# Cosine attention and a GELU layer on one core: a new hand-written order for the first three batches

## The chip, the cores and the metric

The kernel runs on one core of a Trainium2 chip. The core has five engines that run side by side, each through its own instructions in their written order: PE (matrix products; its weight loads are listed apart as PEld), ACT (exponentials, logarithms, GELU, squares), DVE (elementwise work and reductions on vectors), POOL (elementwise work, and the issue of some transfers) and SP (issue of transfers alone). They wait for each other by semaphores. Data lies in an on-chip memory (SBUF); PE writes its results to eight accumulator banks (PSUM), which are used singly or in pairs. The metric is the device time of one execution in microseconds (us).

## The reference

Eight batches of 12 heads, 448 positions, head size 64. Queries and keys are normalised, a softmax over cosines at a temperature of 0.1 weighs the values, and the result goes through a layer with a GELU between two products.

```python
q_n = q / (np.linalg.norm(q, axis=-1, keepdims=True) + 1e-06)
k_n = k / (np.linalg.norm(k, axis=-1, keepdims=True) + 1e-06)
scores = np.matmul(q_n, k_n.transpose(0, 1, 3, 2)) / tau
scores = scores - np.max(scores, axis=-1, keepdims=True)
attn = np.exp(scores)
attn = attn / (np.sum(attn, axis=-1, keepdims=True) + 1e-09)
attn_out = np.matmul(attn, v)
x = attn_out.transpose(0, 2, 1, 3).reshape(B * S, H * D)   # 3584 x 768
h = x @ w_in                                               # 768 x 2048
g = 0.5 * h * (1.0 + erf(h / sqrt(2)))
out = g @ w_out                                            # 2048 x 768
```

## The kernel before

Four heads make a quad, so a batch has three quads: quads 0 to 2 are batch 0, quads 3 to 5 batch 1, quads 6 to 8 batch 2, and so on to 23. A quad's Q and K arrive as one tile `qk` (`load_qk`, on SP). Work on a quad is done by units: unit 0 and unit 1 are the two halves of quad 0, and from there unit n + 1 is quad n. So "quad 1" is unit 2.

A unit passes through these steps, each a small function: `square` (Q or K squared, on ACT, DVE or POOL as the call says), `reduce` (sums of squares, DVE), `logs` and `roots` (a logarithm and an exponential on ACT give the norm), `inverses` (DVE), `scale` (Q or K times the inverse norm, on DVE or POOL), and `transposes`. The latter run on PE with `copies` by DVE behind them for the first units, and as a transposing transfer on SP for later ones. Then `scores` (PE, tile `st`) and `exps` (ACT, tile `pt`) work through a quad in seven chunks, and `sums` and `values` (PE, tiles `sm` and `o`) use them. The sums become reciprocals on DVE (`turned`, `inverted`, `spread`), and `normalise` writes the batch's input `x` of the GELU layer. In place of `sums`, some quads add up their exps on POOL (`folded`) or DVE (`gather`).

The GELU layer of a batch is `mm` or `first` (PE, tiles `hp`: 16 tiles of six products each), `gelu` (ACT, to `g`), and the second product, cut into output pieces of 16 steps (tile `op`). `run(1)` does the next step of the next piece. Steps of a batch's pieces fill PE between the scores of the next batch. `table` loads ACT's set of functions: the exponential set or the GELU set. `spin` issues a filler product that nobody reads.

The weights `wi` come in parts (`load_wi(0)` to `load_wi(3)`, the last two halves of one), `wo` in four, and V in parts; POOL issues these transfers (`load_wi`, `load_wo`, `load_v`) between its other instructions.

What sets the order: for batches 0 to 2 the function `opening` is a list of calls, one line for each step, that fixes the order of every engine's instructions. No scheduler moves them. From the first product of batch 2 on (`first(2)`), loops with a rule for the spacing of scores set the order (`attention`, `first`). Units that share their logarithm and root are in one group (`groups`); units 5 and 6 (quads 4 and 5) are such a pair. `root2` holds the tiles for the roots.

The accumulator pairs `st0` and `st1` alternate between score tiles; `open_third` and `open_fourth` turn single banks into a third and fourth pair once quads 0 to 2 are done.

Of the kernel before, what the change touches and what calls it, by code (L numbers as in the profile page):

```python
# [16 lines left out]
def kernel(  # L17
# [462 lines left out]
    def upto(f, n, last=None):  # L480
        last = {load_qk: NG, load_v: NV, root: len(groups), load_wi: NQ + 1, load_wo: 4}.get(f, NU)
# [56 lines left out]
    def opening():  # L538
        load_qk(0)
        table(EXP_SET)  # L540
        load_qk(1)
        load_qk(2)
        spin(20)
        late_copy()
        load_qk(3)
        x_t[0] = xp.tile([128, KD, S], BF16, tag="x", name="x0")
        square(0, ((AC, Q),))
        square(0, ((AC, K),))
        reduce(0, Q)
        reduce(0, K)  # L550
        square(1, ((AC, Q),))
        load_v(0)
        logs(0)
        reduce(1, Q)
        roots(0)
        load_wi(0)
        square(1, ((AC, K),))
        inverses(0)
        square(2, ((AC, Q),))
        reduce(1, K)  # L560
        scale(0, ((GP, 1),))
        logs(1)
        reduce(2, Q)
        roots(1)
        scale(0, ((GP, 0),))
        spin(2)
        transposes(0, 1)
        square(2, ((AC, K),))
        inverses(1)
        spin(1)  # L570
        transposes(0, 0)
        square(3, ((AC, Q),))
        copies(0, 1)
        scale(1, ((GP, 0),))
        copies(0, 0)
        square(3, ((AC, K),))
        scale(1, ((GP, 1),))
        load_qk(4)
        spin(1)
        transposes(1, 0)  # L580
        reduce(2, K)
        scores(0, ((0, 0), (0, 1)))
        load_v(1)
        transposes(1, 1)
        copies(1, 0)
        logs(2)
        scores(0, ((0, 2), (0, 3)))
        roots(2)
        load_wi(1)
        exps(0, ((0, 0), (0, 1)))  # L590
        inverses(2)
        copies(1, 1)
        exps(0, ((0, 2), (0, 3)))
        spin(2)
        scores(0, ((0, 4), (0, 5)))
        scale(2, ((GP, 0),))
        reduce(3, Q)
        exps(0, ((0, 4), (0, 5)))
        spin(1)
        scores(0, ((1, 0), (1, 1)))  # L600
        reduce(3, K)
        exps(0, ((1, 0), (1, 1)))
        spin(1)
# [12 lines left out]
        exps(0, ((1, 4), (1, 5)))
        inverses(3)
        sums(0, (1,))
        scale(3, ((GP, 0),))
        copies(2, 1)  # L620
        sums(0, (2,))
        exps(0, ((0, 6), (1, 6)))
        sums(0, (3,))
        sums(0, (4,))
        scores(1, ((0, 0), (1, 0)))
        scores(1, ((0, 1), (1, 1)))
        sums(0, (5,))
        exps(1, ((0, 0), (1, 0)))
        sums(0, (6,))
        load_wi(2)  # L630
        transposes(3, 0)
        turned(0)
        exps(1, ((0, 1), (1, 1)))
        scores(1, ((0, 2), (1, 2)))
        values(0, (0,))
        scale(3, ((GP, 1),))
        load_wi(3)
        copies(3, 0)
        values(0, (1,))
# [3 lines left out]
        inverted(0)
        values(0, (3,))
        values(0, (4,))
        spread(0, 1)
        values(0, (5,))
        exps(1, ((0, 3), (1, 3)))
        scores(1, ((0, 4), (1, 4)))
        values(0, (6,))  # L650
        spread(0, 0)
        sums(1, (0,))
        square(4, ((GP, K),))
        exps(1, ((0, 4), (1, 4)))
        sums(1, (1,))
        scores(1, ((0, 5), (1, 5)))
        normalise(0, 0)
        transposes(3, 1)
        exps(1, ((0, 5), (1, 5)))
        scores(1, ((0, 6), (1, 6)))  # L660
        copies(3, 1)
        sums(1, (2,))
        square(4, ((GP, Q),))
        square(5, ((GP, Q),))
        square(5, ((GP, K),))
        load_wo(0)
        load_wo(1)
        exps(1, ((0, 6), (1, 6)))
        sums(1, (3,))
        sums(1, (4,))  # L670
        normalise(0, 1)
        scores(2, ((0, 0), (1, 0)))
        sums(1, (5,))
        exps(2, ((0, 0), (1, 0)))
        sums(1, (6,))
        scores(2, ((0, 1), (1, 1)))
        turned(1)
        values(1, (0,))
        values(1, (1,))
        exps(2, ((0, 1), (1, 1)))  # L680
        values(1, (2,))
        scores(2, ((0, 2), (1, 2)))
        inverted(1)
        values(1, (3,))
        values(1, (4,))
        spread(1, 0)
        values(1, (5,))
        exps(2, ((0, 2), (1, 2)))
        values(1, (6,))
        scores(2, ((0, 3), (1, 3)))  # L690
        sums(2, (0,))
        reduce(4, K)
        normalise(1, 0)
        exps(2, ((0, 3), (1, 3)))
        sums(2, (1,))
        scores(2, ((0, 4), (1, 4)))
        spread(1, 1)
        sums(2, (2,))
        scores(2, ((0, 5), (1, 5)))
        exps(2, ((0, 4), (1, 4)))  # L700
        values(2, (0,))
        values(2, (1,))
        exps(2, ((0, 5), (1, 5)))
        values(2, (2,))
        bank(0, 4)
        bank(0, 5)
        values(2, (3,))
        values(2, (4,))
        scores(2, ((0, 6), (1, 6)))
        exps(2, ((0, 6), (1, 6)))  # L710
        banks(0, 0, 1)
        mm(0, 4, 0, 2)
        sums(2, (3,))
        normalise(1, 1)
        square(6, ((GP, Q),))
        reduce(5, Q)
        reduce(4, Q)
        logs(4)
        sums(2, (4,))
        sums(2, (5,))  # L720
# [715 lines left out]
```

## Time and profile before

| what | value |
|---|---|
| median of 3 runs | 391.53 us |
| lowest and highest run | 390.82 and 393.38 us |
| profiled execution, span from first to last instruction (its only time in the profile) | 390.6 us |
| ACT's last exp of quad 2 ends | 32.42 us |
| batch 0's first product goes on without a break from | 33.3 us |
| batch 1's first product begins | 77.8 us |
| batch 2's first product begins | 129.9 us |

The profile has one line for each group of instructions: line of the code, engine, operation, what it writes and reads, count, and after the bar the busy time in all, the mean of one in nanoseconds, and the engine's idle time ahead of them with what ended it. A row of the timeline gives the start and the length in microseconds, the instruction, how many are merged in it, and in brackets the idle time before it. A row of the stretches gives the window, its length, and then busy time and count for PE, PEld, DVE, ACT and POOL, the granted clock, the share of the transfer engines, and GB/s. A row of the list of waits gives who waited for whom, the total, how often, and the longest.

### The profile page before, as it was taken

What the parts mean: (1) busy time and instruction counts of PE and PEld (TensorE: products, weight loads), DVE (VectorE), ACT (ScalarE), POOL (GpSimd) and SP (SyncE); (2) the same over time, 40 slices, a digit from 0 to 9 for tenths busy, and PEclk for the clock granted to TensorE, in tenths of its full rate; (3) what the DMA queues carried; (4) which work ended last, traced back from release to release, by engine and by line L of the source; (5) the groups of instructions that cost most, each with busy time, mean ns of one, the idle gap of its engine ahead of it and who ended that gap; (6) DMA issues with size and microseconds to landing.
All of it is one profiled execution on the core that took longest, in us unless ns stands there. A gap on an engine that the chain in (4) does not pass through costs nothing.

```text
span 390.6 us, 13166 instructions
## 1 busy us (share of the span) xinstructions
PE 382.6 (98%) x5820; PEld 236.6 (61%) x5820; DVE 273.0 (70%) x509; ACT 269.9 (69%) x391; POOL 248.7 (64%) x161
## 2 busy tenths in 40 slices
PE   7899999999999999999999999999999999999996
PEld 3444568555777656865567556775567555655674
DVE  4878439876778896879696896889685993670032
ACT  5895789857999958996678767997577646504300
POOL 4796950557998399969594794969595770910000
PEclk9999999999999999999999999999999999999999
DMA  8999999926899691889067490876045600130033
GB/s 265 264 262 229 176 191 329 254 56 157 179 203 299 112 217 69 185 158 275 5 172 130 120 243 2 185 131 118 3 91 81 154 9 2 44 82 2 7 79 83
DMA packets 64473, 54.85 MB, mean 140 GB/s; under 512 B 38688, under 2 KB 60320, under 8 KB 64416
## 3 DMA queue, kind: packets, MB, share of 16 engines
q1 hardware_dynamic: 54464, 41.79, 42.0%
q0 software_dynamic: 9568, 11.80, 18.5%
q8 instruction: 45, 0.74, 0.8%
q10 hardware_dynamic: 384, 0.43, 0.4%
q14 instruction: 12, 0.10, 0.1%
HBM read 45.61 MB, written 11.01 MB: 145 GB/s over the span
## 4 chain that ended last, share of the span: by engine, by line
PE 95%; DMA 2%; SPq 1%; ACT 1%; issue 0%; DVE 0%; ACTq 0%
PE hp L493 37%; PE op L427 36%; PE st L257 9%; PE o L346 8%; DMA qk<-in_k_dram 2%; PE op L451 1%; PE sm L323 1%; PE sm L332 1%; PE tp L236 1%; SPq L134 1%; ACT sq L173 0%; ACT pt L267 0%; PE spin L489 0%; DVE last L454 0%; ACT root L195 0%
## 5 line engine op out<-in xcount | busy, mean ns | idle before, releaser
L427 PE MATMUL op<-wo,g 64*64 64x384 bf16 x3456 | 167.1, 323 | 0.2 <-issue 0.2
L267 ACT ACTIVATE pt<-st 128x896 bf16<-128x896 f32 x168 | 147.2, 918 | 19.6 <-PE st L257 17.5
L493 PE MATMUL hp<-x,wi 128*128 128x448 bf16 x768 | 147.0, 353 | 0.0
L427 PEld LDWEIGHTS <-g 64*64 64x64 bf16 x3456 | 106.2, 107 | 40.9 <-issue 4.2
L493 PEld LDWEIGHTS <-wi 128*128 128x128 bf16 x768 | 74.3, 98 | 71.6 <-issue 3.2
L219 POOL TENSOR_TENSOR qkb<-qk,rn 128x896 bf16<-128x896 f32 (+1 forms) x49 | 80.4, 1662 | 46.0 <-DVE rn L203 37.9
L278 POOL TENSOR_TENSOR acc<-acc,pt 128x896 f32<-128x896 f32 x55 | 103.8, 1888 | 4.3
L436 DVE TENSOR_REDUCE ot<-op 128x384 f32<-128x768 f32 x50 | 47.3, 946 | 54.7 <-PE op L427 47.5
L1357 ACT ACTIVATE g<-hp 128x448 bf16<-128x448 f32 x96 | 46.2, 547 | 55.1 <-PE hp L493 55.1
L257 PE MATMUL st<-qkT 64*64 64x448 bf16 x672 | 62.8, 352 | 0.5 <-ACT pt L267 0.5
L183 DVE TENSOR_REDUCE nq<-sq 128x14 f32<-128x896 f32 (+1 forms) x50 | 50.4, 1036 | 13.6 <-ACT sq L173 7.1
L380 DVE TENSOR_TENSOR x<-o,rs 128x448 bf16<-128x448 f32 x48 | 27.6, 611 | 22.9 <-PE o L346 21.9
L175 POOL TENSOR_TENSOR sq<-qk 128x896 f32<-128x896 f32 x16 | 26.6, 1685 | 23.8 <-DMA qk<-in_q_dram 13.3
L346 PE MATMUL o<-pt,v 64*64 64x448 bf16 x672 | 39.5, 349 | 0.0
L290 DVE TENSOR_TENSOR acc<-acc,pt 128x896 f32<-128x896 f32 x30 | 33.0, 1099 | 1.0
L173 ACT ACTIVATE sq<-qk 128x896 f32<-128x896 f32 (+1 forms) x33 | 28.8, 901 | 4.4 <-DMA qk<-in_q_dram 3.2
L257 PEld LDWEIGHTS <-qkT 64*64 64x64 bf16 x672 | 23.1, 106 | 11.7 <-issue 3.7
L375 DVE STREAM_TRANSPOSE rs<-rc 128x448 f32<-128x448 f32 x48 | 28.1, 621 | 0.4
L278 POOL TENSOR_TENSOR acc<-pt 128x896 f32<-128x896 bf16 x11 | 20.7, 1878 | 10.9 <-ACT pt L267 10.9
L346 PEld LDWEIGHTS <-v 64*64 64x64 bf16 x672 | 21.1, 107 | 9.2 <-issue 0.2
L522 ACT ACTIVATE g<-hp 128x448 bf16<-128x448 f32 x32 | 15.4, 547 | 12.8 <-PE hp L493 12.7
L295 DVE TRANSPOSE_TENSOR_REDUCE sa<-acc 128x28 f32<-128x896 f32 x17 | 18.8, 1104 | 0.2
(54 smaller groups left out, 176.0 us busy)
## 6 DMA issues: line engine op xcount, KB each, us to landing
qk<-in_q_dram SPq DMA_DIRECT2D x23, 448.0 KB, 4.9
qk<-in_k_dram SPq DMA_DIRECT2D x23, 448.0 KB, 5.8
out_dram<-ot SPq DMA_DIRECT2D x48, 192.0 KB, 4.0
v<-in_v_dram POOLq DMA_DIRECT2D x6, 672.0 KB, 7.2
wo<-in_moe_w_out_dram POOLq DMA_DIRECT2D x4, 768.0 KB, 10.6
wi<-in_moe_w_in_dram POOLq DMA_DIRECT2D x4, 512.0 KB, 13.8
out_dram<-ot SPq DMA_DIRECT2D x12, 96.0 KB, 2.1
wi<-in_moe_w_in_dram POOLq DMA_DIRECT2D x4, 256.0 KB, 14.1
```

Of the source, the lines that this page charges most:

```text
L173: eng.activation(sq, t, AF.Square)
L183: nc.vector.tensor_reduce(nq_t[n][:, j, i], sq_t[g, i][:, s0:s1], mybir.AxisListType.X, ALU.add)
L219: eng.tensor_tensor(qkb[:, i, :, s0:s1].rearrange("p c s d -> p s c d"), t[:, i, s0:s1], rn[:, i].to_broadcast([128, s1 - s0, C, D]), ALU. ...
L257: nc.tensor.matmul(st[cols, n, :S], lhsT=qkT[rows, 1, c, cols], rhs=qkT[rows, 0, :, cols], start=True, stop=True, tile_position=(64 * s, 6 ...
L267: nc.scalar.activation(pt, st[:, :, :S], AF.Exp, scale=inv_tau)
L278: nc.gpsimd.tensor_tensor(acc_t[g], all_t[g][:, 0] if c == 1 else acc_t[g], all_t[g][:, c], ALU.add)
L290: nc.vector.tensor_tensor(acc_t[g], acc_t[g], all_t[g][:, c], ALU.add)
L346: nc.tensor.matmul(bank_t[g, h][cols, :S], lhsT=v_t[g][rows, s, c, :], rhs=pt_t[g, s, c][rows], start=(c == 0), stop=(c == C - 1), tile_po ...
L427: nc.tensor.matmul(ps[cols, r, :NH], lhsT=g_t[sb][rows, kf, t * 128 + 64 * c:t * 128 + 64 * (c + 1)], rhs=wo[rows, kf, ni * NH:(ni + 1) * NH],
L436: nc.vector.tensor_reduce(part, ps[:, :, :NH].rearrange("p r d -> p d r"), mybir.AxisListType.X, ALU.add)
L493: nc.tensor.matmul(t, lhsT=wi[:, kd, m * 128:(m + 1) * 128], rhs=x_t[b][:, kd, :], start=(kd == 0), stop=(kd == KD - 1))
L1357: nc.scalar.activation(g_t[sb][:, m, hf * S:(hf + 1) * S], hps.pop(m), AF.Gelu)
```

## The change

The list in `opening` is written anew from end to end. Beside the order, the engine of several squares and scalings differs. Four smaller edits are in the code:

- `groups` has unit 6 (quad 5) in a group of its own, the last one, with its own root tile; the loops stop at `NR` groups.
- `gate(4)` takes quad 4's `qk` tile early and lets POOL write one column of it, so that SP's load of quad 4 waits for that instruction.
- `gather` takes the engine (DVE or POOL).
- batch 0's first two output pieces run in turn: 12 steps of one, 12 of the other, then the last 4 of each.

```diff
+    root2 += [consts.tile([128, 4 * C, 2], F32, name=f"root6_{n}") for n in range(1)]
...
+    groups[NQ + 2] = [NQ + 2]
+    NR = len(groups)
+    groups.append([NQ + 3])
...
-        t = qkp.tile([128, 2, 2, C, D], F32, tag="qk", name=f"qk{g}")
+        t = qk_t[g] if g in qk_t else qkp.tile([128, 2, 2, C, D], F32, tag="qk", name=f"qk{g}")
...
+    def gate(g):
+        qk_t[g] = qkp.tile([128, 2, 2, C, D], F32, tag="qk", name=f"qk{g}")
+        nc.gpsimd.memset(qk_t[g][:, :, 0, 0, 0:1], 0.0)
...
-        sr_t[n] = root2[2 if len(groups[n]) == 2 else n % 2][:, :math.prod(shapes[n])]
+        sr_t[n] = root2[3 if n == NR else 2 if len(groups[n]) == 2 else n % 2][:, :math.prod(shapes[n])]
...
-    def gather(g, c):
-        if c == 1:
-            acc_t[g] = accp.tile([128, 2, S], F32, tag="acc", name=f"acc{g}")
-        nc.vector.tensor_tensor(acc_t[g], all_t[g][:, 0] if c == 1 else acc_t[g], all_t[g][:, c], ALU.add)
+    def gather(g, parts):
+        (eng, c), = parts
+        if c == 1:
+            pool, tag, name = (sqp, "sq", f"sq{g}_2") if g == NQ + 1 else (accp, "acc", f"acc{g}")
+            acc_t[g] = pool.tile([128, 2, S], F32, tag=tag, name=name)
+        eng.tensor_tensor(acc_t[g], all_t[g][:, 0] if c == 1 else acc_t[g], all_t[g][:, c], ALU.add)
...
-        square(0, ((AC, Q),))
...
+        square(0, ((DV, Q),))
...
-        fill = [f for t, ni in todo if t not in tail for f in second_pieces(sb, t, ni)]
+        pieces = [second_pieces(sb, t, ni) for t, ni in todo if t not in tail]
+        if b == 0:
+            n = KF * 3 // 4
+            one, two = pieces[:2]
+            pieces[:2] = [one[:n] + two[:n] + one[n:] + two[n:]]
+        fill = [f for p in pieces for f in p]
```

How the new list moves instructions is seen where the engines' rows stand. ACT in the opening, from the log of quad 0's second half to quad 0's first exp (`sq` is a square, `lq` a log, `root` a root, `pt` an exp; of the tiles, 139 and 142 are quads 1 and 2 before, 152 and 199 after). Before:

```order
L190 ACTIVATE lq_199<-nq_184,tiny 128x14
L195 ACTIVATE root_1_126<-lq_199 128x14
L173 ACTIVATE sq_1_217<-qk_139 128x896
L173 ACTIVATE sq_0_233<-qk_142 128x896
L173 ACTIVATE sq_1_238<-qk_142 128x896
L190 ACTIVATE lq_271<-nq_201,tiny 128x28
L195 ACTIVATE root_0_125<-lq_271 128x28
L267 ACTIVATE pt_281<-st_0_255 128x2x448
```

ACT at the same place now:

```order
L198 ACTIVATE lq_196<-nq_155,tiny 128x14
L203 ACTIVATE root_1_126<-lq_196 128x14
L181 ACTIVATE sq_0_235<-qk_152 128x896
L181 ACTIVATE sq_1_239<-qk_152 128x896
L275 ACTIVATE pt_241<-st_2_218 128x2x448
L181 ACTIVATE sq_0_250<-qk_199 128x896
L198 ACTIVATE lq_265<-nq_237,tiny 128x28
L203 ACTIVATE root_0_125<-lq_265 128x28
L275 ACTIVATE pt_241<-st_0_227 128x2x448
```

Both squares of quad 1 now stand behind this log, the K square of quad 2 has left ACT, and an exp stands ahead of quad 1's log. Earlier in ACT's row the table load of the exponential set has moved behind the first square, which brings a table load of its own.

DVE around the copies of quad 0's second half and the inverse norms of quad 1 (`rn_285` before, `rn_271` after). Before:

```order
L241 COPY qkT_208<-tp_0_246 64x896
L201 TENSOR_REDUCE se_283<-root_0_125 128x28
L203 RECIPROCAL rn_285<-se_283 128x28
L241 COPY qkT_208<-tp_1_262 64x896
L183 TENSOR_REDUCE nq_299<-sq_0_233 128x14
L183 TENSOR_REDUCE nq_299<-sq_1_238 128x14
```

DVE at the same place now:

```order
L249 COPY qkT_186<-tp_0_254 64x896
L209 TENSOR_REDUCE se_269<-root_0_125 128x28
L211 RECIPROCAL rn_271<-se_269 128x28
L249 COPY qkT_186<-tp_1_275 64x896
L227 TENSOR_TENSOR qkb_273<-qk_152,rn_271 128x2x7x64
L191 TENSOR_REDUCE nq_303<-sq_0_250 128x14
L191 TENSOR_REDUCE nq_303<-sq_1_244 128x14
```

The scaling of quad 1's K stands on DVE, ahead of the two reduces of quad 2; it was POOL's before.

POOL from the scalings of quad 0's second half on (`wi` and `wo` rows are issues of weight transfers). Before:

```order
L219 TENSOR_TENSOR qkb_197<-qk_133,rn_221 128x7x64 x2
L155 DMA v_260<-in_v_dram 128x4x448
L467 DMA wi<-in_moe_w_in_dram 64x2x2048 x2
L219 TENSOR_TENSOR qkb_297<-qk_139,rn_285 128x2x7x64 x2
L219 TENSOR_TENSOR qkb_364<-qk_142,rn_360 128x2x7x64
L467 DMA wi<-in_moe_w_in_dram 64x2x1024 x2
```

POOL from the same scalings on now:

```order
L227 TENSOR_TENSOR qkb_161<-qk_135,rn_225 128x7x64 x2
L183 TENSOR_TENSOR sq_1_244<-qk_199 128x896
L1518 COPY late<-qk_135 128x1
L227 TENSOR_TENSOR qkb_273<-qk_152,rn_271 128x2x7x64
L477 DMA wi<-in_moe_w_in_dram 64x2x2048 x2
L477 DMA wi<-in_moe_w_in_dram 64x2x1024 x4
L483 DMA wo<-in_moe_w_out_dram 128x4x768
L183 TENSOR_TENSOR sq_1_542<-qk_536 128x896
L145 MEMSET qk_544 128x2
```

POOL squares quad 2's K, scales only quad 1's Q, and issues the first wi part, both last wi parts and a wo part in a row behind it; `load_wi(1)` stands ahead of these rows and `load_wi(0)` is the first wi row here. The last row is the gate that SP's load of quad 4 waits for.

Of the other engines: DVE also scales quad 2's Q and K, the K of quads 3 and 5, and the Q of quads 7 and 8; POOL squares quad 9's K and all of quad 12. In the rows of DVE, all reciprocals and normalisations of quads 0 to 2 stand behind the last copy of quad 2. PE has 24 filler products in place of 28 and otherwise the same instructions.

More of the change, by code (lines that the diff above doesn't have):

```diff
@@ L558, in opening @@
-        inverses(0)
+        table(EXP_SET)
+        logs(0)
+        square(1, ((GP, Q),))
+        roots(0)
+        load_qk(1)
+        reduce(1, Q)
+        inverses(0)
+        scale(0, ((DV, K),))
+        spin(20)
+        square(1, ((AC, K),))
+        reduce(1, K)
+        transposes(0, 1)
+        copies(0, 1)
+        logs(1)
+        roots(1)
+        load_qk(2)
+        load_v(0)
+        load_v(1)
+        scale(0, ((GP, Q),))
+        transposes(0, 0)
+        copies(0, 0)
+        load_wi(1)
@@ L559, in opening @@
+        scores(0, ((0, 2), (0, 3)))
+        inverses(1)
+        scores(0, ((0, 0), (0, 1)))
+        scale(1, ((GP, Q),))
+        spin(1)
         square(2, ((AC, Q),))
-        reduce(1, K)
-        scale(0, ((GP, 1),))
-        logs(1)
         reduce(2, Q)
[L564 to L567, printed above, removed]
         square(2, ((AC, K),))
-        inverses(1)
+        exps(0, ((0, 2), (0, 3)))
+        scale(1, ((GP, K),))
+        square(3, ((GP, K),))
@@ L643, in opening @@
[L643 to L672, printed above, removed]
+        scale(3, ((DV, Q),))
+        values(0, (0,))
+        values(0, (1,))
+        values(0, (2,))
+        values(0, (3,))
+        scores(1, ((0, 2), (1, 2)))
+        copies(3, 1)
@@ new lines, in opening @@
+        turned(0)
+        transposes(3, 0)
+        scores(1, ((0, 4), (1, 4)))
+        sums(1, (0,))
+        sums(1, (1,))
+        bank(0, 5)
+        copies(3, 0)
+        scores(1, ((0, 6), (1, 6)))
+        values(0, (4,))
+        values(0, (5,))
+        values(0, (6,))
+        exps(1, ((0, 2), (1, 2)))
+        exps(1, ((0, 4), (1, 4)))
+        exps(1, ((0, 6), (1, 6)))
+        scores(2, ((0, 0), (1, 0)))
+        sums(1, (2,))
+        sums(1, (3,))
+        banks(1, 2, 0)
+        scores(2, ((0, 1), (1, 1)))
@@ L689, in opening @@
-        values(1, (6,))
-        scores(2, ((0, 3), (1, 3)))
+        values(1, (2,))
+        values(1, (3,))
+        scores(2, ((0, 2), (1, 2)))
+        values(1, (4,))
+        values(1, (5,))
+        values(1, (6,))
+        load_wi(3)
+        load_qk(3)
+        exps(2, ((0, 0), (1, 0)))
+        load_wo(0)
+        square(4, ((GP, K),))
+        gate(4)
+        banks(0, 8, 0)
+        more(0)
+        load_wo(1)
+        scores(2, ((0, 4), (1, 4)))
+        square(4, ((GP, Q),))
+        load_wo(2)
@@ L792, in opening @@
-        gelu(0, 8)
-        gelu(0, 6)
-        copies(4, 1)
-        load_v(2)
-        run(3)
+        gelu(0, 2)
+        scale(4, ((GP, Q),))
+        bank(0, 13)
+        gelu(0, 14)
+        square(6, ((GP, Q),))
+        gelu(0, 12)
+        transposes(4, 1)
+        reduce(6, Q)
+        open_third()
+        square(5, ((GP, K),))
+        reduce(5, K)
+        square(6, ((GP, K),))
+        mm(0, 1, 4, 6)
+        load_wo(3)
+        mm(0, 8, 0, 6)
+        mm(0, 15, 0, 6)
+        transposes(4, 0)
@@ new lines, in opening @@
+        mm(0, 6, 0, 6)
+        gelu(0, 10)
+        gelu(0, 1)
+        gelu(0, 0)
+        gelu(0, 8)
+        table(EXP_SET)
+        logs(5)
+        copies(4, 1)
+        reduce(6, K)
+        logs(19)
+        roots(19)
+        roots(5)
+        mm(0, 7, 0, 6)
+        copies(4, 0)
+        mm(0, 11, 0, 6)
+        inverses(5)
+        inverses(19)
+        open_fourth()
+        mm(0, 9, 0, 6)
+        mm(0, 13, 0, 6)
+        run(1)
+        run(1)
+        run(1)
+        run(1)
+        banks(1, 0, 1)
@@ L847, in opening @@
         run(1)
+        run(1)
+        run(1)
+        run(1)
+        scores(4, ((0, 2), (1, 2)), 1)
+        square(9, ((GP, Q),))
+        square(8, ((GP, K),))
+        exps(4, ((0, 2), (1, 2)))
+        run(1)
+        run(1)
+        gather(3, ((DV, 6),))
+        run(1)
+        run(1)
+        run(1, AC)
+        scores(4, ((0, 1), (1, 1)), 0)
+        run(1)
+        run(1)
+        run(1)
+        run(1)
+        run(1)
+        scores(4, ((0, 4), (1, 4)), 1)
+        exps(4, ((0, 1), (1, 1)))
@@ L1030, in opening @@
-        run(5)
+        table(EXP_SET)
+        logs(7)
+        logs(8)
+        roots(7)
+        roots(8)
+        table(GELU_SET)
+        gelu(1, 4)
+        gelu(1, 6)
+        gelu(1, 11)
+        gelu(1, 7)
+        gelu(1, 10)
+        gelu(1, 9)
+        gelu(1, 8)
+        gelu(1, 12)
+        gelu(1, 13)
+        gelu(1, 14)
+        gelu(1, 15)
+        inverses(7)
+        scale(8, ((DV, Q),))
+        transposes(7)
+        load_qk(10)
+        load_qk(11)
+        scale(8, ((GP, K),))
@@ L1361, in first @@
             nc.scalar.preload_act_table_set(EXP_SET)
-            due = [n for n in range(done.get(root, 0), 2 * b + 8) if n < len(groups)]
+            due = [n for n in range(done.get(root, 0), 2 * b + 8) if n < NR]
             for n in due:
```

923 lines of the change are left out of this document (475 added, 448 removed).

## The prediction

> **What bounds the kernel now.** I read the page's first parts and the chain of work that ended last, then the table of stretches, PE's list of waits, and last the timelines of ACT, DVE and POOL in the opening.
>
> ```profile
> span 390.6 us, 13166 instructions
> PE 382.6 (98%) x5820; PEld 236.6 (61%) x5820; DVE 273.0 (70%) x509; ACT 269.9 (69%) x391; POOL 248.7 (64%) x161
> PEclk9999999999999999999999999999999999999999
> PE 95%; DMA 2%; SPq 1%; ACT 1%; issue 0%; DVE 0%; ACTq 0%
> ```
>
> PE is the bound: 95% of the chain, at a full clock. The stretches (PE's busy time is the first number behind the length) tell where it is not:
>
> ```profile
> 8.90:33.30 24.40, 22.67 (x275) 10.76 (x276) 19.58 (x34) 21.99 (x31) 21.83 (x20) 1.00 1.10 265
> 33.30:130.00 96.70, 96.51 (x1561) 62.38 (x1558) 68.85 (x128) 79.33 (x117) 63.59 (x40) 1.00 0.92 204
> ```
>
> ```profile
> PE spin L489 <- DVE qkT L241: 0.9, 1, 0.9
> PE st L257 <- ACT pt L267: 0.5, 1, 0.5
> PE op L427 <- issue: 0.2, 1, 0.2
> ```
>
> From 33.3 to 130 us PE rests 0.2 us. So the batches that the change reorders cannot become much shorter; the instructions are the same but for 24 filler matmuls in place of 28. What can be won lies ahead of 33.3 us, where PE rests, runs fillers (spin) and works on quads 0 to 2 at the pace at which ACT delivers exps:
>
> ```profile
> 1.18 1.28 ACT L501 ACT_TABLE_LOAD   x1 [1.18 <-PEq L1417]
> 4.54 1.51 ACT L173 ACTIVATE sq<-qk 128x448 f32<-128x448 f32 x3 [2.08 <-DMA qk<-in_q_dram]
> 6.33 0.31 ACT L190 ACTIVATE lq<-nq,tiny 128x14 f32<-128x14 f32 x1 [0.28 <-DVE nq L183]
> ...
> 8.35 0.95 ACT L173 ACTIVATE sq<-qk 128x896 f32<-128x896 f32 x1 [1.00 <-DMA qk<-in_q_dram]
> 9.21 0.29 ACT L190 ACTIVATE lq<-nq,tiny 128x14 f32<-128x14 f32 x1
> ...
> 12.66 0.95 ACT L173 ACTIVATE sq<-qk 128x896 f32<-128x896 f32 x1 [0.97 <-DMA qk<-in_k_dram]
> 13.52 0.30 ACT L190 ACTIVATE lq<-nq,tiny 128x28 f32<-128x28 f32 x1
> ...
> 13.99 4.13 ACT L267 ACTIVATE pt<-st 128x896 bf16<-128x896 f32 x5
> ...
> 20.35 12.07 ACT L267 ACTIVATE pt<-st 128x896 bf16<-128x896 f32 x14 [0.16 <-PE st L257]
> ```
>
> From 13.99 to 32.42 ACT has one gap, 0.16 us. Its last 14 exps (quads 1 and 2) take 12.07 us, 0.862 each, and PE follows at once:
>
> ```profile
> 32.78 0.57 PE L346 MATMUL o<-pt,v 64*64 64x448 bf16 x8
> ```
>
> ```profile
> 33.35 13.35 PE hp L493 x70
> 129.96 18.27 PE hp L493 x96
> ```
>
> So the start of batch 0's first product (hp) is the time of quad 1's first exp, 20.35 us, plus 12.07, plus about 0.9. I lay the opening out anew up to that exp.
>
> **The change part by part.** Durations in the opening, DVE and POOL:
>
> ```profile
> 5.15 1.67 DVE L183 TENSOR_REDUCE nq<-sq 128x7 f32<-128x448 f32 x3 [3.12 <-ACT sq L173]
> ```
>
> ```profile
> L434 DVE TENSOR_TENSOR ot<-ot,op 128x384 f32<-128x384 f32 x4 | 2.2, 550 | 0.2
> L219 DVE TENSOR_TENSOR qkb<-qk,rn 128x896 bf16<-128x896 f32 x1 | 1.1, 1092 | 0.0
> L183 DVE TENSOR_REDUCE nq<-sq 128x14 f32<-128x896 f32 x46 | 48.1, 1073 | 10.5 <-POOL sq L175 6.4 <-ACT sq L173 3.9
> L436 DVE TENSOR_REDUCE ot<-op 128x384 f32<-128x768 f32 x50 | 47.3, 946 | 54.7 <-PE op L427 47.5 <-ACT pt L267 7.0
> L219 POOL TENSOR_TENSOR qkb<-qk,rn 128x448 bf16<-128x448 f32 x4 | 3.7, 951 | 1.1 <-DVE rn L203 1.1
> L175 POOL TENSOR_TENSOR sq<-qk 128x896 f32<-128x896 f32 x16 | 26.6, 1685 | 23.8 <-DMA qk<-in_q_dram 13.3 <-DVE nq L183 7.4 <-DMA qk<-in_k_dram 2.1
> ```
>
> 1. Quad 0, first half. Its K is squared by ACT, its Q by DVE: no row has DVE on 448 columns, so 0.55 (384 columns) to 1.09 (896); I take 0.6. Q lands at 4.5, is squared by 5.15, two reduces of 0.56 end at 6.3: the log starts at 6.35, as before (6.33). The second table load, 1.28 us, fits in between, behind the square that ends at 4.9.
>
> 2. The K scaling goes from POOL (0.95) to DVE (0.6), and the second half's Q square to POOL, so the second half's log comes at 8.65 instead of 9.21. Behind it ACT issues both squares of quad 1, an exp, and the Q square of quad 2, 0.86 each. The K square of quad 2, which waited for its DMA until 12.66, is on POOL now. Quad 1's log waits for DVE: inverses of the second half until 10.65 (POOL scales Q at 8.05, PE and DVE turn it by 10.15), two reduces of 1.05, so 12.75 instead of 13.52, with one of quad 0's seven exps already done.
>
> 3. Four exps follow from 13.2. DVE: copy, inverses (done 13.9), copy, then the K scaling of quad 1, 14.5 to 15.6, in front of the reduces of quad 2, 17.65. ACT is through with what it may do at 17.5, so log and root of quad 2 end by 18.1, quad 0's last exp at 19.0, and quad 1's first exp starts there: 1.35 us earlier than 20.35. The rest of the chain is 14 exps as before; the scores, sums and values beside them fit between. I keep **1.2 us** of it, since the normalisations of quads 0 to 2 now all stand late in DVE's row and end at about 36.0, against a need at about 36.1. Bounds: 0 and 1.35.
>
> 4. The loads. SP's loads of quad 4, which went out as soon as quad 0 was scaled, wait behind a POOL memset that itself stands behind three weight parts: they issue at about 23. Behind them on SP is only quad 5's load, then nothing before 53 us. Who waits for them is POOL (quad 4's Q square, from about 28 on), in front of a DVE reduce at 36: 8 us of slack. POOL's weight loads wait for free DMA slots, and the squares of quad 3 behind them are needed by DVE at 28.7, ready at 25.4. The second wi part is loaded first, the first one behind the scaling of quad 1. Nothing, unless it lands late (second rival).
>
> 5. Batches 0 to 2. The same matmuls in another order, at PE's limit: from hp to batch 2's hp 96.6 us before, with 0.2 of waits. The first two output pieces in turn need the late gelus 12 steps later and cost at most the eviction of the first piece, 0.95 us against the 1.03 us of PE work in front of the third piece: nothing. The roots of quad 5 apart add a log, a root and two inverse steps, about 0.35 us on ACT and 0.3 on DVE, neither at its limit there. New waits are possible at three narrow places, worked out with the rows' durations: quad 4's first scores are due at 60.0 and its transposes land at 60.05 (they go last behind three POOL scalings and take up to 6.3, below); quad 5's normalised x ends 0.35 us ahead of PE, because a reduce that waits for POOL stands in front of it; batch 2's third bank pair is due at 131.3 and quad 8's normalisation, behind POOL's six folds, ends at 131.5. I take 0.2 in all, which replaces the old 0.2: **0**. Bounds: -0.2 and +2.
>
> ```profile
> DMA to landing us min/median/max: 4.0/5.1/6.3
> ```
>
> ```profile
> 6.65 1.22 POOL L467 DMA_DIRECT2D wi<-in_moe_w_in_dram  x2
> ```
>
> ```profile
> DMA to landing us min/median/max: 10.0/14.1/17.3
> ```
>
> (The first row is that of the transposes, the second the issue of the first wi part, the third the landing of all wi parts.)
>
> Sum: 390.6 - 1.2 + 0 = 389.4 of span. The runs' median, 391.53, is 0.9 above the profiled span, the lowest run, 390.82, 0.2 above. So **390.3 us**, a gain of 0.3%.
>
> **The rivals.**
>
> First: DVE and POOL exclude each other. At 14.5 us two scalings of quad 1 become ready together, K on DVE (14.5) and Q on POOL (14.4, behind its square and a small copy). In this trace POOL is held up by DVE:
>
> ```profile
> L161 POOL COPY then<-pt 128x1 bf16<-128x1 bf16 x1 | 1.1, 1127 | 4.2 <-ACT pt L267 4.2
> ```
>
> ```profile
> 87.84 1.09 DVE L219 TENSOR_TENSOR qkb<-qk,rn 128x896 bf16<-128x896 f32 x1
> 90.33 1.10 DVE L175 TENSOR_TENSOR sq<-qk 128x896 f32<-128x896 f32 x1
> 87.89 6.74 POOL L219 TENSOR_TENSOR qkb<-qk,rn 128x896 bf16<-128x896 f32 x3 [0.38 <-DVE rn L203]
> ```
>
> Three POOL instructions of this size take 5.06 us alone (3 x 1.685); beside a DVE scaling and a DVE square they took 6.74, 1.7 more, and a copy of one column took 1.1. In each of these DVE began first or at once. That DVE waits when POOL began first no row shows: 0 to 1.7 us. If it does, and POOL wins, the DVE scaling ends at 17.2, quad 2's reduces at 19.3, and quad 1's first exp starts at about 20.75, 0.4 later than before: 391.9 us. If DVE wins, POOL's Q scaling ends at 17.2 and PE's second transposes of quad 1 still come before DVE's copy at 18.2: the forecast. The Trainium skill, page "SBUF — State Buffer", section "SBUF: two separate sides", states it both ways: a DVE instruction with two SBUF inputs and a POOL instruction that reads SBUF lock each other out for a whole instruction, and who comes first decides. The trace agrees for one direction, with 6.74 us in place of 5.06; by that rule this rival's time holds whenever POOL is first.
>
> Second, on the other side: the first wi part lands late. It was issued at 6.65 us and is now issued behind the Q scaling, at about 17.2 and 17.85. PE needs it at 31.7, as the first thing in hp. With the longest wi row, 17.3 us, it lands at 35.1; PE stands for 3.4 us, the gain is gone and 393.7 comes out. It is worse than before from a landing at 33 on, and by over 1% from 36.8 on. Against it: with the median of 14.1 it lands at 32.0, and less is in front of it, since the loads of quads 4 and 5 no longer compete before 23 us.
>
> Third: more comes out than I count, the waits inside the batches shrink and the whole 1.35 us arrives: 388.8. Against it stands PE's 0.2 us of rest: there is nothing more to win.
>
> **How the numbers follow.** Forecast 0.5; first rival 0.25, it is a matter of 0.1 us; second 0.12, half of it over 1%; third 0.05; other narrow places summing to 1 to 5 us, 0.08. The range takes in the third (388.8, rounded down to 388.7), the first and nearly the second: 388.7 to 393.5. About 1%, 3.9 us, is what a measurement of this kernel tells from no change. Faster by more needs all of PE's rest in the opening: 0.03. Slower by more: half the second, a part of the rest: 0.09. Within 1%: 0.88.
>
> **What would show it.** Step 1: first log at 6.35. Step 2: quad 1's log at 12.75. Step 3: quad 1's first exp at 19.0 and hp at about 32. Step 5: PE's rest from hp to batch 2's hp below 0.5 us. The first rival shows as a DVE scaling near 14.5 us that takes over 2 us, the second as a PE wait for DMA at the start of hp. I am wrong if ACT has a gap above 0.5 us after 13 us, or if a wait of PE above 1 us stands behind 33 us.

## The result and the profile after

The changed kernel took 397.29 us (median of 4 runs, 395.51 to 400.83), the kernel before 391.79 us beside it: 1.0149 times as long, with a 95% interval of 1.0109 to 1.0188. The forecast was 390.3 us, in a range up to 393.5. The profiled execution of the changed kernel is its longest one, 400.83 us with a span of 399.0. Here and below a median is taken over all runs, and a ratio over the fast ones alone, which leaves out runs more than 1.5% above the fastest of their kernel.

The head of its page (span, busy time by engine, clock in 40 slices, and the chain of work that ended last by engine):

```profile
span 399.0 us, 13173 instructions
PE 384.6 (96%) x5816; PEld 235.8 (59%) x5816; DVE 287.7 (72%) x519; ACT 269.9 (68%) x390; POOL 244.5 (61%) x159
PEclk9978999999999999999999999999999999999999
PE 84%; DVE 10%; issue 2%; POOL 2%; ACT 1%; POOLq 0%; DVEq 0%; ACTq 0%
```

Before, PE had 95% of that chain and DVE 0%; now DVE has 10%, and the clock is below full speed in the third and fourth slice. Where the time came from is read off the starts of each batch's first product (hp) in PE's timeline, first of the changed kernel, then of the kernel before:

```profile
38.54 10.21 PE L503 MATMUL hp<-x,wi 128*128 128x448 bf16 x52
...
84.06 18.61 PE L503 MATMUL hp<-x,wi 128*128 128x448 bf16 x96
...
138.50 18.33 PE L503 MATMUL hp<-x,wi 128*128 128x448 bf16 x96
```

```profile
77.69 18.33 PE L493 MATMUL hp<-x,wi 128*128 128x448 bf16 x96
```

With 33.3 and 129.9 us for batches 0 and 2 before (quoted above), batch 0 begins 5.2 us later, lasts 1.1 us longer (45.5 against 44.4, of which 0.4 is only two products that stood ahead of it before), and batch 1 lasts 2.2 us longer (54.4 against 52.2). From batch 2 on nothing changes: 8.6 us late there, 8.4 at the end.

The list of PE's waits names them:

```profile
PE tp L244 <- DVE qkb L227: 3.1, 3, 2.0
...
PE op L437 <- issue: 1.1, 1, 1.1
PE st L265 <- DVE qkT L249: 1.6, 2, 0.9
PE tp L244 <- DVE qkT L249: 1.0, 1, 1.0
PE st L265 <- issue: 0.9, 1, 0.9
```

PE waits for scalings by DVE (qkb), of which the list had none before. DVE's three scalings of a whole quad, and what POOL does meanwhile:

```profile
14.38 2.30 DVE L227 TENSOR_TENSOR qkb<-qk,rn 128x896 bf16<-128x896 f32 x1
...
20.37 5.74 DVE L227 TENSOR_TENSOR qkb<-qk,rn 128x896 bf16<-128x896 f32 x2
```

```profile
14.05 1.68 POOL L227 TENSOR_TENSOR qkb<-qk,rn 128x896 bf16<-128x896 f32 x1
...
20.20 0.76 POOL L483 DMA_DIRECT2D wo<-in_moe_w_out_dram  x1 [0.90 <-DMA wi<-in_moe_w_in_dram]
20.96 1.70 POOL L183 TENSOR_TENSOR sq<-qk 128x896 f32<-128x896 f32 x1
...
23.45 1.71 POOL L183 TENSOR_TENSOR sq<-qk 128x896 f32<-128x896 f32 x1
```

A scaling takes DVE 1.09 us. The first one (quad 1's K) took 2.30: it ends at 16.68, 0.95 behind the end of POOL's scaling (quad 1's Q), as if it had begun only about then. The two of quad 2 took 5.74 us instead of 2.2, beside POOL's two squares of quad 3. POOL's own instructions have their usual 1.7 us. ACT, which paced the opening, shows what followed:

```profile
12.37 0.32 ACT L198 ACTIVATE lq<-nq,tiny 128x28 f32<-128x28 f32 x1
...
18.70 0.32 ACT L198 ACTIVATE lq<-nq,tiny 128x28 f32<-128x28 f32 x1 [1.34 <-DVE nq L191]
...
20.34 2.54 ACT L275 ACTIVATE pt<-st 128x896 bf16<-128x896 f32 x3 [0.26 <-PE st L265]
24.61 0.92 ACT L275 ACTIVATE pt<-st 128x896 bf16<-128x896 f32 x1 [1.74 <-PE st L265]
```

Quad 1's log comes even earlier than forecast (12.37 against 12.75), quad 2's log a microsecond late (18.70 against 17.65), quad 1's first exp at 20.34 as before, and then ACT runs dry, since PE's row has quad 2's transposes ahead of quad 1's later scores. The stretch behind it (the fraction near the end of the row is the granted clock):

```profile
25.20:31.90 6.70, 5.72 (x51) 2.04 (x43) 4.68 (x8) 3.91 (x5) 1.90 (x2) 0.50 1.09 254
```

For these 6.7 us PE ran at half its clock. In batch 1, PE has two pauses in which it waited for nothing that the profile shows:

```profile
127.87 0.35 PE L437 MATMUL op<-wo,g 64*64 64x384 bf16 x3 [1.12 <-issue]
...
134.34 0.38 PE L265 MATMUL st<-qkT 64*64 64x448 bf16 x3 [0.89 <-issue]
```

So there are three suspects: DVE and POOL shutting each other out, the half clock, and these pauses.

### The profile page after: what moved, and what is told of

The parts are those of the page before. It is cut to its first block, busy times and chain, and to the rows that moved or that the text cites. A ratio compares the mean times of both kernels' runs of the same rounds, so it can differ in the third digit from the quotient of the medians.

```text
span 399.0 us, 13173 instructions
## 1 busy us (share of the span) xinstructions
PE 384.6 (96%) x5816; PEld 235.8 (59%) x5816; DVE 287.7 (72%) x519; ACT 269.9 (68%) x390; POOL 244.5 (61%) x159
## 4 chain that ended last, share of the span: by engine, by line
PE 84%; DVE 10%; issue 2%; POOL 2%; ACT 1%; POOLq 0%; DVEq 0%; ACTq 0%
PE hp L503 33%; PE op L437 33%; PE st L265 7%; PE o L356 7%; DVE qkb L227 2%; DVE nq L191 2%; DVE acc L293 1%; PE op L461 1%; PE sm L333 1%; DVE qkT L249 1%; DVE x L390 1%; DVE rs L385 1%; PE tp L244 1%; POOL qkb L227 1%; POOL sq L183 1%
## 5 line engine op out<-in xcount | busy, mean ns | idle before, releaser
L227 POOL TENSOR_TENSOR qkb<-qk,rn 128x896 bf16<-128x896 f32 (+1 forms) x42 | 69.9, 1685 | 65.3 <-DVE rn L211 54.6
L265 PE MATMUL st<-qkT 64*64 64x448 bf16 x672 | 65.3, 357 | 3.0 <-DVE qkT L249 1.6
L183 POOL TENSOR_TENSOR sq<-qk 128x896 f32<-128x896 f32 (+1 forms) x19 | 32.3, 1710 | 20.4 <-DMA qk<-in_q_dram 19.2
L181 ACT ACTIVATE sq<-qk 128x896 f32<-128x896 f32 (+1 forms) x29 | 25.8, 920 | 2.1 <-DMA qk<-in_k_dram 1.9
```

The lines of the kernel that those rows point to most:

```text
L183: eng.tensor_tensor(sq, t, t, ALU.mult)
L227: eng.tensor_tensor(qkb[:, i, :, s0:s1].rearrange("p c s d -> p s c d"), t[:, i, s0:s1], rn[:, i].to_broadcast([128, s1 - s0, C, D]), ALU. ...
L265: nc.tensor.matmul(st[cols, n, :S], lhsT=qkT[rows, 1, c, cols], rhs=qkT[rows, 0, :, cols], start=True, stop=True, tile_position=(64 * s, 6 ...
```

## The experiments

Twelve runs: the changed kernel again and eleven further kernels, on several chips. The table has the median of each with its ratio to the kernel before on the same chip, and, from each one's profiled execution, the start of batch 0's first product, the length of batches 0 and 1 (from first product to first product), the time at half clock, and the sum of PE's pauses put down to issue behind 100 us.

| kernel | median us | ratio, 95% interval | hp of batch 0 | batch 0 | batch 1 | half clock | pauses |
|---|---|---|---|---|---|---|---|
| before (profile above) | 391.79 | 1 | 33.3 | 44.4 | 52.2 | 0 | 0.2 |
| changed | 397.29 | 1.0149, 1.0109 to 1.0188 | 38.5 | 45.5 | 54.4 | 6.8 | 2.0 |
| again: changed, once more | 397.05 | 1.013, 1.010 to 1.016 | 35.2 | 45.6 | 53.4 | 6.8 | 0.9 |
| hold: POOL's squares wait | 394.75 | 1.009, 1.007 to 1.011 | 33.0 | 45.6 | 52.7 | 3.4 | 0.5 |
| poolk: quad 1's K on POOL | 396.07 | 1.012, 1.008 to 1.017 | 34.8 | 45.3 | 53.0 | 3.4 | 0.5 |
| spins: 14 late fillers | 399.31 | 1.019, 1.014 to 1.023 | 36.2 | 45.6 | 53.2 | 0 | 0.8 |
| fewer: before, 24 fillers | 392.58 | 0.999, 0.994 to 1.003 | 31.8 | 44.8 | 52.0 | 0 | 0 |
| lockfill: 6 early fillers | 395.64 | 1.008, 1.004 to 1.013 | 36.3 | 45.6 | 53.9 | 0 | 1.4 |
| fill: hold and 6 fillers | 393.34 | 1.003, 1.000 to 1.006 | 32.9 | 45.6 | 52.4 | 0 | 0.3 |
| parts: fill and three edits | 391.44 | 0.999, 0.996 to 1.002 | 31.9 | 45.2 | 51.9 | 0 | 0 |
| morefill: before, 34 fillers | 392.97 | 1.002, 0.999 to 1.005 | 32.7 | 44.7 | 52.9 | 0 | 0.9 |
| nofill: parts, 24 fillers | 392.90 | 1.003, 0.999 to 1.006 | 34.8 | 45.2 | 51.9 | 6.8 | 0 |
| latev: V load behind folds | 394.13 | 1.006, 1.002 to 1.009 | 34.0 | 45.6 | 51.9 | 0 | 0 |
| seq: parts, pieces in a row | 391.40 | 1.000, 0.998 to 1.003 | 31.7 | 45.2 | 52.1 | 0 | 0 |

### The changed kernel again

> The changed kernel once more, for a second profile and a ratio beside the next three. Both theories of the opening (locks between DVE and POOL, or the new row order itself) expect the same picture as in the first profile: DVE scalings of 2.3 us near 14.4 us and of 3.3 and 2.6 us from 20.4 us on, a clock of 0.5 from about 25.5 to 32 us, the first hp of batch 0 at 38.5 us (0.3 either way), and a time 1% to 2% above the kernel before. The two pauses of PE behind 126 and 133 us (1.1 and 0.9 us, put down to issue) are a matter of chance if they are late loads of PE's code: then they differ from the first profile by over 0.5 us in all; if they belong to the new order they come back at the same matmuls with the same length.

The ratio came back, the picture not: the half clock lay from 16.9 to 23.7 us, the scalings of quad 2 took 1.09 and 2.57 us (DVE won the first time), and hp came at 35.2. PE paused once, for 0.9 us, at the first of the two matmuls, in place of 2.0 us at both. So how much each of the three suspects takes differs from one execution to the next; what counts are medians and parts that are taken away.

### Keeping POOL out of DVE's way

```diff
+    def hold():
+        stay = nrm.tile([128, 1], BF16, tag="stay", name="stay", bufs=1)
+        nc.gpsimd.tensor_copy(stay, qkb_t[2][:, Q, C - 1, 1, D - 1:D])
...
         load_wo(0)
+        hold()
         square(4, ((GP, K),))
```

> POOL's two squares of quad 3 wait for DVE's second scaling of quad 2 (a one-column copy on POOL in front of them reads its result). Lock theory: DVE's two scalings near 20.4 us take 1.1 us each, the transposes of quad 2 start by 21.6 instead of 23.7, ACT has no gap above 0.6 us, the clock stays at 1.0, and the first hp of batch 0 comes at 33.3 to 34 instead of 38.5: some 5 us less than the changed kernel, level with the kernel before within 1%. The scaling near 14.4 us stays at 2.3. Order theory (PE's new row, with quad 2's transposes in front of quad 1's later scores, is late by itself): hp at 36 or later, under 3 us less.

DVE's timeline, and POOL's:

```profile
14.38 1.11 DVE L227 TENSOR_TENSOR qkb<-qk,rn 128x896 bf16<-128x896 f32 x1
...
20.15 2.09 DVE L227 TENSOR_TENSOR qkb<-qk,rn 128x896 bf16<-128x896 f32 x2
```

```profile
14.50 2.54 POOL L227 TENSOR_TENSOR qkb<-qk,rn 128x896 bf16<-128x896 f32 x1
```

Quad 2's scalings are back at 1.05 us each, and hp comes at 33.0: the order theory (36 or later) falls. At 14.4 us DVE came 0.12 us ahead of POOL in this execution, and now POOL waited, 2.54 us for 1.68 us of work. This is the exclusion in both directions, which the kernel before could show in one only. The Trainium skill, page "SBUF — State Buffer", section "SBUF: two separate sides", has it so; by it and by these rows alike, the first comer keeps the other out for its whole instruction. (The last section has rows in which DVE came first and was held all the same.)

The median fell by 2.3 us against "again", not by 5, and the clock was not full:

```profile
16.20:19.60 3.40, 3.40 (x24) 1.88 (x24) 2.50 (x5) 2.62 (x5) 3.40 (x6) 0.52 1.11 214
```

That part of the expectation was wrong, and it made the clock a cause of its own.

### The K scaling of quad 1 on POOL

```diff
         scale(2, ((GP, Q),))
+        scale(2, ((GP, K),))
...
-        scale(2, ((DV, K),))
```

> The K scaling of quad 1 on POOL behind the Q scaling, instead of on DVE. Lock theory: POOL has it from 15.7 to 17.4; DVE's reduces of quad 2 start at 14.4 instead of 16.6, their log comes at about 16.6 to 17.5 instead of 18.7, the scalings of quad 2 on DVE are done by about 20.5, before POOL's weight issues and squares (from about 21.5) get there, and run 1.1 us each; first hp of batch 0 at 32 to 33.3, 5 to 6 us less than the changed kernel and 0 to 1 us less than the kernel before. Order theory: hp at 36 or later.

A miss. Quad 2's log came at 17.2 as expected, but PE waited for the K scaling until 17.45, its copies on DVE stood ahead of quad 2's inverses, and quad 2's scalings began at 20.2 as ever, into POOL's weight issues and squares: 1.97 and 2.56 us. Freeing DVE earlier did not take its scalings out of POOL's way, since what stood ahead of them came no earlier.

### Fillers where PE waits

```diff
+        spin(9)
         transposes(3, 1)
...
+        spin(5)
         transposes(3, 0)
```

> Nine filler matmuls in front of the first and five in front of the second transposes of quad 2, so that PE is busy while it would wait for DVE. Nothing of the locks changes. Lock theory with the clock as its follow-on: the DVE scalings stay at 2.3, 3.3 and 2.6 us, the clock stays at 1.0 behind 25 us, and PE's matmuls between 26.7 and 32 us take half as long: first hp at 35.5 to 37 instead of 38.5. If the half clock costs nothing, since PE waits for ACT there anyway: hp stays at 38.5 or comes later by the fillers, up to 1 us.

In the profile the clock stayed full and hp came at 36.2, as the first theory had it. The median did not follow: 2.3 us above "again". The other three of its four runs had a mean granted clock of 0.991 to 0.996, so these fillers did not hold it; they stand behind 21 us, and in "again" the clock had fallen at 16.9. Whether they also cost PE time was not tried: at a full clock hp comes no later than in "lockfill" below (36.2 against 36.3).

### The clock by itself, and both together

The kernel before with four of its 28 fillers taken out, the changed kernel with more fillers between 9.4 and 17 us, and the hold with the same fillers. The expectations speak of seven added and 31 in all; the lines below add six, which makes 30 (PE has 5822 matmuls on the page of "lockfill", 5816 on that of the changed kernel):

```diff
+        spin(2)
         scores(0, ((0, 2), (0, 3)))
...
-        spin(1)
+        spin(2)
         scores(0, ((0, 6), (1, 6)))
...
+        spin(2)
         scores(0, ((1, 2), (1, 3)))
...
+        spin(1)
         scores(0, ((1, 0), (1, 1)))
```

> The kernel before with four of its 28 filler matmuls taken out (those between quad 0's scores, 13.9 to 16.5 us); nothing else. Clock theory (the 24 fillers of the changed kernel leave PE too little to do, and the clock halves for 3.4 or 6.8 us): the granted clock falls to 0.5 for 3.4 us or 6.8 us between 14 and 26 us in the profile, the first hp of batch 0 comes 0.5 to 3 us later than 33.3, and the time is 0.2% to 0.8% above the kernel before. Rival (the half clock comes only with the waits for DVE, the number of fillers is free): the clock stays at 1.0, hp at 33.3 within 0.3, same time.

> The changed kernel with seven more fillers between 9.4 and 17 us (31 in all), locks untouched. Lock theory: the clock stays at 1.0 at least up to 22 us, the DVE scalings still take 2.3 us near 14.4 and 3.6 us or more together from 20.4 on unless DVE comes first, and hp of batch 0 stands at 35 to 36.5. If the clock is the whole loss: hp at 32 to 33.3.

> Both: POOL's squares of quad 3 wait for DVE's scalings of quad 2, and seven more fillers. Lock and clock together explain the opening: clock 1.0 throughout, scalings of quad 2 at 1.1 us each, quad 1's first exp at 19.0 to 19.8, hp of batch 0 at 31.7 to 32.6 (kernel before: 33.3). Batch 0 still lasts 45.3 to 45.7 us from hp to hp (before 44.4), batch 1 52.3 to 53.5 (before 52.2), so the time is within 0.3% of the kernel before, some 2 us less than with the hold alone. If something else is wrong in the opening, hp stays above 33.

Each run's mean granted clock is listed with its time. For "fewer", five runs at 0.999 or 1.000 took 391.0 to 391.5 us, and five at 0.983 to 0.990 took 393.7 to 397.1. So with four fillers fewer the old order lost the clock in five of ten runs, against five of 31 of the kernel before beside it. The profiled run was free of it, so what was expected of its profile did not show, and the ratio, 0.999, shows no loss. For "hold", four runs at 0.996 took 393.5 to 394.4, four at 0.991 took 394.7 to 395.4, two at 0.981 and 0.982 took 396.4 and 396.8: a staircase. A mean of 0.996 is 3.4 us at half clock in a span of 392, 0.991 is about 7, and 0.981 about 14. Over all kernels with the new opening and 24 fillers, 33 of 42 runs were below 0.998; of those with 30 fillers, 2 of 42; of the kernel before with its 28, 14 of 87.

"lockfill" came out as the lock theory had it, with a full clock and hp at 36.3. "lockfill" and "fill" differ by the hold alone, and both profiles have a full clock. DVE's timeline in the one, then in the other:

```profile
20.42 5.74 DVE L227 TENSOR_TENSOR qkb<-qk,rn 128x896 bf16<-128x896 f32 x2
```

```profile
20.37 2.09 DVE L227 TENSOR_TENSOR qkb<-qk,rn 128x896 bf16<-128x896 f32 x2
```

The exclusion on quad 2 costs 3.3 us of the opening (36.27 against 32.94) and 2.3 us of the medians. With both gone hp at 32.9 missed the 31.7 to 32.6 expected of "fill": the first exp of quad 1 still came at 20.34, not at 19.0 to 19.8, since the scaling at 14.4 us was held by POOL again, 2.30 us.

### One edit in each stage

```diff
-        scale(2, ((GP, Q),))
+        scale(2, ((GP, K),))
+        scale(2, ((GP, Q),))
...
-        scale(2, ((DV, K),))
...
-        load_v(4)
...
         folded(8, (6,))
+        load_v(4)
...
-            pieces[:2] = [one[:n] + two[:n] + one[n:] + two[n:]]
+            pieces[:2] = [one[:n] + two[:n - 4] + one[n:] + two[n - 4:]]
```

> As the last, and one edit in each stage. Opening: both scalings of quad 1 on POOL, K first; hp of batch 0 at 31.5 to 32.3. Batch 0: the first piece is finished after 12+8 steps instead of 12+12, so that 8 steps lie between its last and the third piece; if the third piece waits for the first one's eviction (0.4 us at 58.6 in the hold run), that wait goes and batch 0 lasts 45.1 to 45.3 instead of 45.6; if it comes from something else, 45.6 stays. Batch 1: the V load of quads 9 to 11 is issued behind POOL's folds (about 126 us instead of 110); if PE's pauses at its 1629th and 1757th matmul are late code loads beside that transfer, their sum falls from 0.7 to 2.5 us to below 0.5 us, and batch 1 lasts 52.0 to 52.3; if not, they stay. In all 390 to 391.5 us, at or just below the kernel before.

All three did as expected. The opening: quad 1's exps start 1.0 us earlier, and without a break from there on (ACT's timeline):

```profile
19.31 11.73 ACT L275 ACTIVATE pt<-st 128x896 bf16<-128x896 f32 x14 [0.40 <-PE st L265]
```

Batch 0: PE at the start of the third piece, in "hold" and here. The eight scores ahead of it have 0.38 us of work; the difference of the starts is 0.68 there and 0.37 here, so the third piece no longer waits for the first one's eviction (in "hold" DVE has that eviction from 58.02 to 58.98, and PE goes on at 59.03):

```profile
58.35 0.58 PE L265 MATMUL st<-qkT 64*64 64x448 bf16 x8
59.03 2.27 PE L437 MATMUL op<-wo,g 64*64 64x384 bf16 x49
```

```profile
56.98 0.58 PE L265 MATMUL st<-qkT 64*64 64x448 bf16 x8
57.35 2.96 PE L437 MATMUL op<-wo,g 64*64 64x384 bf16 x68
```

Batch 1: no pause is left, and it lasts 51.9 us, just below the 52.0 to 52.3 expected. The whole takes what the kernel before takes. Not all exclusion is gone: POOL still holds scalings by DVE in batches 0 and 1 (1.40 us at 36.8, 2.34 at 48.1 and 1.75 at 91.4), but PE's list of waits names none of them.

### Three checks

> The changed kernel with one edit: the V load of quads 9 to 11 behind POOL's folds. Code-load theory: PE's pauses at its 1629th and 1757th matmul (2.5, 1.5 and 2.0 us together in three profiles of this opening) fall below 0.5 us, batch 1 lasts 51.9 to 52.4 us instead of 53.4 to 54.4, and the median falls by 1 to 2 us to 395 to 396. If the pauses have nothing to do with that transfer: they stay between 0.7 and 2.5 us and the median stays at 396.5 to 397.5. The opening is that of the changed kernel: DVE scalings held by POOL, a half clock or none, hp of batch 0 at 35 to 38.5.

The edit is the one of `load_v(4)` alone, in the changed kernel. The pauses went and batch 1 lasted 51.9 us, as expected; the median fell by 3 us, more than the 1 to 2 expected, and one execution with hp at 34.0 does not say why. Not all of it need be the load: six of the ten runs kept a mean clock of 0.998 or more, against one of eight of the changed kernel, on another chip. In the list of waits the pauses ahead of this edit are 2.0 us in the changed kernel, 0.9 in "again" and 1.4 in "lockfill", two of them below the sums in the expectation. POOL issues the load at 116 us in the changed kernel, just ahead of a transposing transfer, two stores and four loads that SP issues from 117 to 125.5 us; before, it stood behind the folds. POOL's timeline in the changed kernel, then before:

```profile
116.31 0.88 POOL L163 DMA_DIRECT2D v<-in_v_dram  x1
```

```profile
125.21 0.88 POOL L155 DMA_DIRECT2D v<-in_v_dram  x1
```

> The last kernel (three edits, one per stage) without the seven added fillers, 24 in all. Clock theory: runs scatter again from 391 to 396, the median is 1 to 3 us above the 391.4 with fillers, and if the profiled run is one of the long ones its clock shows 0.5 for 3.4 or 6.8 us ahead of 33 us. If the fillers do nothing once the locks are gone: 391 to 392 in all runs, clock 1.0.

Eight of ten runs were at 0.990 to 0.994 and took 392.5 to 394.8 us, the two at a full clock 390.9 and 391.2: the fillers are worth about 1.5 us of the median, and nothing in a run that keeps its clock.

> The kernel before with 34 fillers instead of 28 (six more between 9.8 and 16.5 us). Of 31 runs of the kernel before beside the last four kernels ten took 392.9 to 399 us and 21 took 390.3 to 392.3. Clock theory (the half clock also strikes the kernel before now and then): with six more fillers nearly all runs lie between 390.3 and 392.5, as those of the two kernels with 31 fillers did, and the median is 0 to 1 us below the kernel before. If the scatter has another cause: as many runs above 393 as the kernel before beside it.

A miss: the nine runs at a full clock took 391.5 to 393.8 us, 392.86 in the median against 391.43 for the full-clock runs beside them, so six more fillers do not help the old order, and one of ten runs still lost its clock. The ratio, 1.002 with 1 inside its interval, does not tell the two apart. Its profile has quad 1's first exp at 19.83, 1.0 us behind that of "fewer" (18.83), and a pause of 0.9 us in batch 1; whether these are the reason stays open.

### The two pieces in a row

```diff
-            pieces[:2] = [one[:n] + two[:n - 4] + one[n:] + two[n - 4:]]
+            pieces[:2] = [one + two]
```

> The kernel with one edit per stage and 31 fillers, and the first two output pieces one behind the other again instead of in turn. If taking them in turn is worth nothing once the third piece waits no more (the last gelu of batch 0 ended at 51.6 us there, and in a row its first reader would come at about 53.4): batch 0 lasts 45.2 us within 0.2, the time is 391.4 within 0.5, level with the kernel before. If the late gelus are needed earlier than that: batch 0 is 0.5 to 1.5 us longer and the time 392 to 393.

391.40 us, batch 0 in 45.2: taking the pieces in turn was worth nothing, and the one effect of it that the profiles show is the wait of the third piece.

## Why the prediction was wrong

Two terms that the sum left at nothing failed: POOL's squares of quad 3 in step 4, which shut DVE out of quad 2's scalings, and the four fillers fewer, which let the clock fall. The first rival, which did come true in the profile, was given too small a chance and too small a price.

- **Steps 1 and 2** were right: first log at 6.26 (6.35), quad 1's log at 12.37 (12.75).
- **Step 3** failed. It gave quad 1's first exp at 19.0 and hp at about 32. Where nothing of the opening is shut out and the clock is full that is about what comes: 19.31 and 31.9 in "parts", hp at 31.7 in "seq"; but there both scalings of quad 1 stand on POOL. In the changed kernel the scaling at 14.4 us lost its race, as it did in six of the seven profiles that have it on DVE behind that copy (in "hold" POOL lost it), which is the first rival. It put quad 1's first exp at 20.75; that came at 20.34, 1.0 us behind "parts". In "hold", where DVE won, it came at 20.41 all the same, with the half clock from 16.2 us on, so no profile shows the step's own order with the race won at a full clock. That rival had a chance of 0.25, "a matter of 0.1 us"; it should have been the likelier one, since by the step's own times POOL came first (14.4 against 14.5).
- **Step 4** hid the largest term. It set down POOL's squares of quad 3 as nothing, because their reader had 3 us of slack. It asked who waits for these squares, and not whom they shut out. Worked back from its 25.4 us (two squares of 1.69, a weight issue of 0.8 and a memset of 0.1), the first square starts at 21.1. Quad 2's scalings start 1.7 us behind quad 2's log (18.70 to 20.37 above): by the forecast at 19.3, ahead of the squares, but with the first rival's delay at 21.0, into them. The rival was priced at 0.4 us without asking what its delay would run into; the meeting was worth 3.3 us of the opening ("lockfill" against "fill"). In "poolk" scalings and squares met without that delay too.
- **The fillers** had no term at all; the prediction only counted 24 in place of 28 and read "a full clock" off the page. The half clock took 2.3 us of the opening in the profiled execution (38.54 against 36.27 in "lockfill", which differs by six fillers), and about 1.5 us of the medians ("nofill" against "parts").
- **Step 5** gave nothing for the pieces in turn, on 0.95 us of eviction against 1.03 us of PE work. It left out the hand-over at both ends of the eviction; PE waited 0.3 us. The three narrow places that it named (60.0 us, quad 5's x, 131.5 us) brought no wait. The moved V load, worth 0.5 to 2 us in batch 1, was not in the prediction: the transfers of batches 1 and 2 were not followed past SP's.
- **The second rival** did not occur: hp never waited for `wi`. The third rival did not come either; its 388.8 us does not follow from its own terms, since 1.35 and 0.2 us off the median of 391.5 leave 390.0.
- **The gain.** Even with all this taken away the time is that of the kernel before. The base of the sum was a late one: in the profile of before, ACT waits 1.00 us for quad 1's Q and 0.97 us for quad 2's K (its rows at 8.35 and 12.66, quoted in the prediction), while in "fewer", whose order is the same up to there, it squares quad 1's Q at 7.15 and reaches quad 1's first exp at 18.83 instead of 20.35:

```profile
18.83 12.07 ACT L267 ACTIVATE pt<-st 128x896 bf16<-128x896 f32 x14 [0.16 <-PE st L257]
```

  So the forecast gain of 1.2 us is no more than what late loads had added to that one execution, as far as one profile of each can say. The last term of the sum, 0.9 us from span to median, hid it: in every run that lists both, the time is 1.7 to 1.9 us above the span (400.83 and 399.0 in the changed kernel), so the profiled execution of before stands for some 392.4 us, already 0.9 above the median. Another 0.4 us goes in batch 0 (45.2 against 44.4, with the two products counted): PE rests 0.26 us there in "parts" and not at all before. These short waits were not followed.

In medians, the 5.5 us are about 2.3 for the exclusion on quad 2, 1.9 for the three edits of "parts" (by stage, in the profiles, 1.0, 0.4 and 0.6), and 1.7 for the clock (changed against "lockfill"); that sums to 5.9, since "parts" comes out 0.35 below the 391.79 of the kernel before. The first two are from one chip; the 1.7 compares two chips, and by the ratios to the kernel before on each it is 2.5, each ratio with an interval of about 1.6 us either way.

## What to carry to other kernels

For each vector operation that is moved between DVE and POOL, list what the other engine runs at that time, not only who waits for its result: two scalings side by side took nearly as long here as one behind the other (14.05 to 16.68 us, for 1.68 and 1.09 us of work). Fillers that keep PE busy while it waits are part of the schedule; if some are dropped, look at the granted clock of every run, since one profile may miss the loss. And a load that is moved ahead can cost pauses of PE that no wait in the profile explains: here they went when the load was moved back.

## What the runs showed of the hardware

- The clock fell in pieces of 3.4 us (hold, poolk) or 6.8 us (changed, again, nofill), though PE's longest rest in the 3.4 us ahead was 2.0 us in the changed kernel and 0.5 us in "hold". The Trainium skill, page "TensorE: Matmul & The Clock Gate", section "Part 1: The HAM clock gate (the "warmup" mystery)", gives a free-running window of 3413 ns; the pieces and the chance agree. Its rule of an idle window does not: PE was 2.88 us busy in the 3.4 us before the fall in "hold", and just as long from 12.8 to 16.2 us in the kernel before, which kept its clock. (In the changed kernel it was busy for 1.52 of the 3.4 us before the fall.) What told "hold" and the kernel before apart stays open. The row of the stretches of "hold", then of the kernel before:

```profile
12.80:16.20 3.40, 2.88 (x24) 1.14 (x23) 3.20 (x6) 3.25 (x5) 3.40 (x3) 1.00 1.21 262
```

```profile
12.80:16.20 3.40, 2.88 (x24) 1.15 (x22) 2.55 (x5) 3.37 (x6) 3.21 (x4) 1.00 1.05 244
```

- PE's pauses stand behind its 1629th or its 1757th matmul (or both) wherever they came, 128 apart, also in the kernels in which 6 or 14 fillers shift the work under these numbers. The profile page's row of the instruction queue is

```profile
q8 instruction: 45, 0.74, 0.8%
```

  or 16.4 KB each, and PE's 5816 matmuls make 45.4 blocks of 128. That PE waits there for the next block of its code, behind other transfers, fits this and "latev"; it was not shown by itself.
- DVE was also held where it began before POOL's square: at 20.37 us against 20.96 in the changed kernel, with a weight issue of POOL going on. In "again" and "fill" it began 0.04 and 0.06 us behind the start of such an issue, in "nofill" 0.52 us, and took its usual 1.09 us. In "poolk" a scaling that began at 20.18 amid such issues took 1.97 us, though POOL's square began only at 21.68. So an issue seems able to hold DVE, but not each one does; what decides is open.
